# Block-sparse attention followed by a gated feed-forward layer on one core: chunks shifted by one block, opening gathers moved between queues, feed-forward units dealt by cost

## The chip, the cores and the metric

The kernel runs on one core of a Trainium2 chip. The trace names five engines with a stream of instructions each: PE (matrix products, with its weight loads as PEld), DVE (vector work), ACT (activation functions and copies), POOL (GpSimd) and SP, which here only issues transfers. Transfers are issued from the queues of SP, POOL and ACT and moved by 16 DMA engines.

The metric is the device time of one execution in microseconds (us). The kernel before was run three times: 340.7, 341.94 and 342.27 us, with the median 341.94. One further execution was profiled. Its own time was 341.41 us, and 339.6 us of it is the span that the profile shows. All times within the profile count from the start of that span.

## The reference

Inputs are q, k and v of shape (4, 8, 768, 64): 4 batches, 8 heads, 768 positions, 64 wide. A sequence has 24 blocks of 32 positions. A query block sees its own and the two neighbouring blocks, the first block (0), the last block (23), and three blocks drawn for it in `sampled_blocks`. Query blocks 0 and 23 see everything ("global" blocks, both as queries and as keys).

```python
scores = scale * np.matmul(q, k.transpose(0, 1, 3, 2))
mask = np.abs(blk_i - blk_j) <= 1
mask = mask | (blk_i == 0) | (blk_j == 0) | (blk_i == n_blocks - 1) | (blk_j == n_blocks - 1)
for qb in range(n_blocks):
    for kb in sampled_blocks[qb]:
        mask[qb * block:(qb + 1) * block, kb * block:(kb + 1) * block] = True
attn = softmax(np.where(mask, scores, -1e9))
x = np.matmul(attn, v)                  # then (3072, 512): batch and position by head and width
h = x @ w_in                            # (3072, 2048)
g = h * (1.0 / (1.0 + np.exp(-beta * h)))
out = g @ w_out                         # (3072, 512)
```

## The kernel before, in words

**Attention.** A chunk is 128 query positions, four blocks, of one batch; there are 6 chunks a batch and 24 in all. Chunk c holds blocks 4c to 4c+3, so that chunk 0 has the global block 0 and chunk 5 the global block 23. `CHUNK_ORDER` (L47 and below) visits them as 1, 2, 0, 5, 3, 4. A step is one chunk with one half of the heads (Q = 0 or 1, four heads each): 12 steps a batch, 48 steps, listed by hand in `steps`. PE, POOL and SP run in the order in which the program issues to them; DVE and ACT are reordered by a scheduler.

A step computes, for every ordinary block, a score tile of 32 queries by 256 keys: 96 neighbour keys, 32 keys of block 0, 96 drawn keys and 32 keys of block 23. `gather_chunk` lays these 256 keys side by side in a buffer KG (three buffers, `kg_bufs`): the neighbours by L248 (on ACT, on DVE in the opening), the global blocks by L253 and the drawn blocks by L259 (on POOL; the second halves of the first two chunks on DVE). `scores` (L320) multiplies, takes the row maximum on DVE (`nm`, L327) and exponentiates on ACT (`probs`, L330). `probs_T` transposes on PE (L341) and copies on DVE (L345). `attend` multiplies with the values (`av`, L392), normalises on DVE (L410, L411), and `x_transpose` (L434) builds `xT` once both halves of a chunk are done. `do_T` and `do_A` run one and two steps behind the scores.

The values lie in DRAM as a table `vtab` of 16-bit rows with all heads (1,040 bytes each). `gather_v` fetches VA (neighbours and block 0, SP's queue, L281 to L287) and VB (drawn blocks and block 23). Of VB, the blocks named in `direct` come row block by row block from SP (L291 to L297, addresses from registers), the others by an indirect gather from POOL's queue (L278). VA and VB have three buffers each, so the gather for a chunk waits until the chunk three before it has been attended.

Global query blocks are scored against all 768 keys by `global_scores` (L356) and transposed by `global_T` (L378). `attend` then multiplies them in 24 matmuls of 32 columns a step (L404), in the steps of chunk 0 and of chunk 5.

**Feed-forward ("MoE" in the code).** Chunks are collected into groups of 2, 2, 4, 4, 4, 4, 4. An h unit (`h_unit`, L448) makes 128 of the 2,048 inner columns for a group, 16 units a group; ACT takes tanh (L452) and DVE combines (L454). An o unit (`o_unit`, L465) is half of the 16 accumulating matmuls of one chunk's output; the second half is followed by a copy on ACT (L471) and the output DMA (L473). `push_group` queues a group's h units, mixed with the o units held back from earlier groups. The loop over steps deals units between the attention's instructions: as many as the queue holds divided by the steps left until the next group, rounded up.

**Opening.** SP loads k, q and v of batch 0; DVE and ACT cast; `write_vtab` writes the table (SP, 15.79 us). `prefetch_v` then fetches VA and VB of the first two chunks, with one block of each from SP and the other six by indirect gathers from POOL. POOL goes on with the loads of `w_in` (4 pieces), of k, q, v for batch 1 and of `w_out` (4 pieces), between its key copies. In step 3 the program issues two global scores, four `attend`s and the first two h units.

Of the kernel before, what the change touches and what calls it, by code (L numbers as in the profile page):

```python
# [20 lines left out]
def kernel(  # L21
# [26 lines left out]
    CHUNK_ORDER = [1, 2, 0, 5, 3, 4]  # L48
# [106 lines left out]
    def load_regs(t, engine, top, c):  # L155
        i0, i1 = max(4 * c, 1), min(4 * c + 4, NB - 1)
        _, vs = nc.values_load_multi_w_load_instructions(
            t[0:1, 3 * i0:3 * i1], engines=[engine], min_val=0, max_val=top,
            skip_runtime_bounds_check_because="block indices of the sampled blocks")
        return {(i, r): vs[3 * (i - i0) + r] for i in range(i0, i1) for r in range(3)}  # L160
# [78 lines left out]
    def gather_chunk(b, c, KG, p0, p1, eng=None, steady=False):  # L239
        eng = eng or nc.gpsimd  # L240
        js = [j for j in range(4) if 0 < 4 * c + j < NB - 1]
        j0, j1 = js[0], js[-1] + 1
        kv = kT[b]
        k_regs = load_regs(sb_raw, eng.engine, NB - 1, c)
        for w0 in range(p0, p1, 2):
            base = kv[:, w0:w0 + 2, (4 * c + j0 - 1) * BLK:(4 * c + j0 + 2) * BLK]
            ap = list(base.ap)
            (nc.scalar.copy if steady else nc.vector.tensor_copy)(  # L248
                out=KG[:, j0:j1, w0:w0 + 2, 0:96],
                in_=dataclasses.replace(base, ap=[ap[0], [BLK, j1 - j0], ap[1], ap[2]]))  # L250

        for col, src in ((96, 0), (224, S - BLK)) if chunk_seq.index((b, c)) % 6 < 3 else ():
            eng.tensor_copy(  # L253
                out=KG[:, :, p0:p1, col:col + BLK],
                in_=kv[:, p0:p1, src:src + BLK].unsqueeze(1).to_broadcast(
                    [P, 4, p1 - p0, BLK]))
        for j in js:
            for r in range(3):
                eng.tensor_copy(  # L259
                    out=KG[:, j, p0:p1, 128 + BLK * r:160 + BLK * r],  # L260
                    in_=kv[:, p0:p1, bass.ds(k_regs[(4 * c + j, r)] * BLK, BLK)])

    def gather_v(b, c, direct=()):
# [3 lines left out]
        js = [j for j in range(4) if 0 < 4 * c + j < NB - 1]  # L267
# [8 lines left out]
        for j in js:  # L276
            if j not in direct:
                nc.gpsimd.indirect_dma_start(  # L278
                    VB[:, j, :], None, tab[:, :],
                    bass.IndirectOffsetOnAxis(idx_b[:, 4 * c + j:4 * c + j + 1], 0))  # L280
        nc.sync.dma_start(out=VA[0:96, js[0]:js[0] + nj, :],  # L281
                          in_=rows((4 * c + js[0] - 1) * BLK, 96, BLK, nj))
        ga = [j for j in js if 4 * c + j != 1]
        nc.sync.dma_start(out=VA[96:128, ga[0]:ga[0] + len(ga), :],
                          in_=rows(0, BLK, 0, len(ga)))
        if len(ga) != nj:
            nc.sync.dma_start(out=VA[96:128, 1, :], in_=tab[S:S + BLK, :])  # L287
        if direct:
            v_regs = load_regs(sb_eff, ET.SP, NB, c)
            gb = [j for j in direct if 4 * c + j != NB - 2]  # L290
            nc.sync.dma_start(out=VB[96:128, gb[0]:gb[0] + len(gb), :],  # L291
                              in_=rows(S - BLK, BLK, 0, len(gb)))
            if len(gb) != len(direct):
                nc.sync.dma_start(out=VB[96:128, NB - 2 - 4 * c, :], in_=tab[S:S + BLK, :])
            for j in direct:
                for r in range(3):
                    nc.sync.dma_start(  # L297
                        out=VB[BLK * r:BLK * (r + 1), j, :],
                        in_=tab[bass.ds(v_regs[(4 * c + j, r)] * BLK, BLK), :])
# [3 lines left out]
    def scores(b, c, Q, KG):  # L303
# [6 lines left out]
        for hp in range(2):  # L310
            for pr in range(2):
                pg = 2 * Q + pr
                for j in range(4):
                    i = 4 * c + j
                    rr = slice(64 * hp, 64 * hp + 64)
                    if 0 < i < NB - 1:
                        rhs = KG[rr, j, pg, :]
                    else:
                        rhs = kT[b][rr, pg, 0:256]
                    nc.tensor.matmul(scs[hp][BLK * j:BLK * (j + 1), pr, :],  # L320
                                     lhsT=qT[b][rr, pg, i * BLK:(i + 1) * BLK],
                                     rhs=rhs, start=True, stop=True,
                                     tile_position=(64 * hp, BLK * j))
# [24 lines left out]
    def global_scores(b, Q, hp):  # L348
        rr = slice(64 * hp, 64 * hp + 64)
        halves = []  # L350
        for s in range(2):
            sct = ring.tile([P, 512], FP32, tag="bank", name="scg")[:, 0:384]
            halves.append(sct)
            for j in range(4):
                pr, blk = j // 2, (j % 2) * (NB - 1)
# [28 lines left out]
    def attend(b, c, Q, ptT, VA, VB, gTs, x16):  # L384
        av = ring.tile([P, 512], FP32, tag="bank", name="av")[:, 0:4 * VW].rearrange(
            "p (u e) -> p u e", e=VW)
        js = [j for j in range(4) if 0 < 4 * c + j < NB - 1]
# [9 lines left out]
        if len(js) < 4:  # L397
            j = 0 if c == 0 else 3
            bi = 0 if c == 0 else 1
            for u in range(4):  # L400
                pr, hp = u // 2, u % 2
                jj = 2 * pr + bi
                for ct in range(6):
                    nc.tensor.matmul(av[BLK * j:BLK * (j + 1), u, :],  # L404
                                     lhsT=gTs[hp][:, ct, BLK * jj:BLK * (jj + 1)],
                                     rhs=v16[b][:, ct, 4 * Q + u, :],
                                     start=(ct == 0), stop=(ct == 5),
                                     tile_position=(0, BLK * j))
# [51 lines left out]
    def o_unit(gi, s, part):  # L460
# [7 lines left out]
        if part == 1:  # L468
# [3 lines left out]
            r0 = b * S + c * P  # L472
            nc.scalar.dma_start(out=out[r0:r0 + P, :], in_=osb)  # L473
# [28 lines left out]


    steps = []
    for b in range(B):
        for (c, Q) in ((1, 0), (2, 0), (1, 1), (2, 1), (0, 0), (5, 0), (0, 1), (5, 1),
                       (3, 0), (3, 1), (4, 0), (4, 1)):
# [3 lines left out]
    def prep_items(b):  # L511
# [13 lines left out]
        if b == 1:  # L525
# [8 lines left out]
            for a in range(4):  # L534
                trs[5 + a] += [tr("kkqq"[a], a % 2, 0), tr("kkqq"[a], a % 2, 1)]
# [32 lines left out]
    def gather_values(n):  # L568
        if n < len(chunk_seq):
            b, c = chunk_seq[n]  # L570
            if b == 0:
                direct = {0: (1, 2, 3), 5: (0, 1, 2)}
            else:
                direct = {0: (1, 2), 5: (0, 1)}
# [25 lines left out]
    prefetch_v(0, (3,))  # L600
    prefetch_v(1, (3,))
# [42 lines left out]

    for n, (b, c, Q) in enumerate(steps):
        sidx = n % SPB
        if sidx == 0:
            prep = prep_items(b + 1) if b + 1 < B else None
        if next_group < len(groups):
            need = sum(sizes[:next_group + 1])  # L650
            gap = max(1, 2 * need + 2 - n)
        else:
            gap = max(1, len(steps) - n)
        units = -(-len(moe_q) // gap)
        pt = scores(b, c, Q, KGs[(b, c)])
        pend_T.append((b, c, Q, pt))
# [5 lines left out]
        elif n == 1:  # L662
# [4 lines left out]
            kg_half(0, 1, nc.vector)  # L667
            load_w_in(0)
# [3 lines left out]
        elif n == 2:  # L672
            do_T()
            kg_half(1, 1, nc.vector)
            load_w_in(2)
            load_w_in(3)
        elif n == 3:
# [4 lines left out]
            do_G(0, 0)  # L682
# [4 lines left out]
            do_GT()  # L687
            do_A()
            do_G(0, 1)
            do_A()  # L690
            do_X()
            do_GT()
            st_v1.append(big("st_v1"))
            run_moe(2)
# [28 lines left out]
        if n > SPB and 2 <= sidx <= 5:  # L723
            acts.append((0.55, lambda: do_G(b, sidx - 2)))
        elif n in (4, 5):
            acts.append((0.55, lambda: do_G(b, n - 2)))
        if pend_X:
            acts.append((0.85, do_X))
        done = 0
        for share, f in sorted(acts, key=lambda a: a[0]):  # L730
            upto = int(units * share + 0.5)
            run_moe(upto - done)
            done = upto
            f()
        run_moe(units - done)
# [44 lines left out]
```

## Time and profile before

| | |
|---|---|
| median of three runs | 341.94 us |
| the profiled execution | 341.41 us, of which 339.6 us are the span |
| PE busy | 292.8 us (86%), 4,288 matmuls |
| DVE, ACT, POOL busy | 222.4, 225.7, 174.3 us |
| DMA | 56.95 MB, 168 GB/s over the span |
| granted TensorE clock | 0.979 of full speed over the span |

The costliest groups of instructions, with the line, the engine, the operation, `out<-in`, the count, busy time in all and mean ns of one, and the idle time of the engine before them:

```profile
L448 PE MATMUL hps<-xT,w_in_sb 128*128 128x512 f16 (+1 forms) x448 | 99.2, 360 | 1.9 <-DVE gnm L366 0.7
L465 PE MATMUL ops<-w_out_sb,g 128*128 128x512 f16 x384 | 89.6, 379 | 3.8 <-DMA w_out_sb<-in_moe_w_out_dram 3.8
L259 POOL COPY KG<-kT 128x128 f16 (+1 forms) x264 | 62.8, 293 | 3.0 <-PE sc L320 1.9
L248 ACT COPY KG<-kT 128x768 f16<-128x768 f16 (+1 forms) x44 | 34.6, 793 | 11.3 <-PE sc L320 7.1
```

The mean of a matmul counts its way through the pipeline: eight matmuls of 512 columns in a row take 1.73 us, not eight times 360 ns. A slice of the page is 339.6 / 40 = 8.5 us.

### The profile page before, as it was taken

What the parts mean: (1) busy time and instruction counts of PE and PEld (TensorE: products, weight loads), DVE (VectorE), ACT (ScalarE), POOL (GpSimd) and SP (SyncE); (2) the same over time, 40 slices, a digit from 0 to 9 for tenths busy, and PEclk for the clock granted to TensorE, in tenths of its full rate; (3) what the DMA queues carried; (4) which work ended last, traced back from release to release, by engine and by line L of the source; (5) the groups of instructions that cost most, each with busy time, mean ns of one, the idle gap of its engine ahead of it and who ended that gap; (6) DMA issues with size and microseconds to landing.
All of it is one profiled execution on the core that took longest, in us unless ns stands there. A gap on an engine that the chain in (4) does not pass through costs nothing.

```text
span 339.6 us, 11327 instructions
## 1 busy us (share of the span) xinstructions
PE 292.8 (86%) x4288; PEld 166.1 (49%) x4288; DVE 222.4 (65%) x506; ACT 225.7 (66%) x447; POOL 174.3 (51%) x451
## 2 busy tenths in 40 slices
PE   0554898669787999887999999999989999899995
PEld 0342556545555565544455565454555554444442
DVE  3666878624859777899686668677997576534400
ACT  1693579943768799887688987667776545335411
POOL 5659985629889955879696519725131200000000
PEclk9999999979969999999799999999999999999999
DMA  6979999997698992659898327724162510000021
GB/s 169 377 230 202 292 252 326 274 225 239 169 286 207 314 268 51 173 137 294 183 306 251 75 68 191 178 59 115 35 184 68 135 57 33 31 33 31 32 93 64
DMA packets 40135, 56.95 MB, mean 168 GB/s; under 512 B 7280, under 2 KB 31984, under 8 KB 40080
## 3 DMA queue, kind: packets, MB, share of 16 engines
q0 software_dynamic: 10160, 26.21, 29.2%
q1 hardware_dynamic: 24400, 23.71, 25.7%
q10 hardware_dynamic: 5520, 6.30, 5.4%
q8 instruction: 34, 0.56, 0.7%
q14 instruction: 21, 0.17, 0.2%
HBM read 50.77 MB, written 9.62 MB: 178 GB/s over the span
## 4 chain that ended last, share of the span: by engine, by line
PE 57%; DVE 14%; DMA 10%; ACT 10%; issue 3%; POOL 3%; SPq 1%; another core or an unknown queue 0%; POOLq 0%; DVEq 0%; ACTq 0%
PE ops L465 21%; PE hps L448 19%; PE tp_p L341 5%; ACT probs L330 5%; DVE nm L327 4%; DVE g L454 4%; DMA w_out_sb<-in_moe_w_out_dram 4%; DMA st_kq<-in_k_dram 4%; PE sc L320 3%; PE av L392 3%; DMA st_q<-in_q_dram 3%; ACT t_sb L452 2%; PE av L404 2%; DVE gnm L364 2%; PE tp_x L434 1%
## 5 line engine op out<-in xcount | busy, mean ns | idle before, releaser
L448 PE MATMUL hps<-xT,w_in_sb 128*128 128x512 f16 (+1 forms) x448 | 99.2, 360 | 1.9 <-DVE gnm L366 0.7
L454 DVE SCALAR_TENSOR_TENSOR g<-t_sb,hps 128x512 f16<-128x512 f16 (+1 forms) x112 | 66.8, 609 | 46.9 <-ACT t_sb L452 44.2
L465 PE MATMUL ops<-w_out_sb,g 128*128 128x512 f16 x384 | 89.6, 379 | 3.8 <-DMA w_out_sb<-in_moe_w_out_dram 3.8
L452 ACT ACTIVATE t_sb<-hps,beta_h_sb 128x512 f16<-128x512 f32 (+1 forms) x112 | 70.3, 647 | 29.4 <-PE hps L448 26.4
L330 ACT ACTIVATE probs<-sc,nm 128x256 f16<-128x256 f32 x192 | 76.9, 485 | 18.2 <-DVE nm L327 14.3
L327 DVE TENSOR_REDUCE nm<-sc 128x2 f32<-128x512 f32 x96 | 62.9, 684 | 20.0 <-PE sc L320 16.5
L278 POOL DMA_INDIRECT VB<-vtab,idx_b x40 | 38.9, 972 | 71.5 <-PE av L392 55.9
L259 POOL COPY KG<-kT 128x128 f16 (+1 forms) x264 | 62.8, 293 | 3.0 <-PE sc L320 1.9
L448 PEld LDWEIGHTS <-w_in_sb 128*128 128x128 f16 x448 | 42.8, 101 | 35.3 <-issue 5.2
L465 PEld LDWEIGHTS <-g 128*128 128x128 f16 x384 | 36.8, 98 | 45.8 <-issue 4.7
L248 ACT COPY KG<-kT 128x768 f16<-128x768 f16 (+1 forms) x44 | 34.6, 793 | 11.3 <-PE sc L320 7.1
L345 DVE COPY probsT<-tp_p 128x1024 f16<-128x1024 f16 x48 | 32.3, 673 | 4.8 <-PE hps L448 1.7
L341 PE MATMUL tp_p<-identity,probs 128*128 128x128 f16 x384 | 32.2, 231 | 1.2 <-ACT probs L330 0.6
L471 ACT ACTIVATE osb<-ops 128x512 f32<-128x512 f32 x24 | 14.4, 601 | 28.0 <-PE ops L465 27.9
L320 PE MATMUL sc<-KG,qT 64*32 64x256 f16 x704 | 25.0, 294 | 7.5 <-DVE KG L259 5.1
L341 PEld LDWEIGHTS <-probs 128*128 128x128 f16 x384 | 23.9, 103 | 5.2 <-issue 2.0
L392 PEld LDWEIGHTS <-probsT 128*32 128x32 f16 x1408 | 17.4, 100 | 18.1 <-issue 14.1
L369 ACT ACTIVATE gp<-scg,gnm 128x384 f16<-128x384 f32 x32 | 16.9, 581 | 13.7 <-DVE gnm L366 7.5
L392 PE MATMUL av<-VA,probsT 128*32 128x65 f16 x704 | 22.1, 203 | 2.8 <-issue 2.7
L392 PE MATMUL av<-VB,probsT 128*32 128x65 f16 x704 | 21.8, 201 | 2.9 <-DMA VB<-vtab 2.2
L411 DVE TENSOR_TENSOR x<-av,rec 128x256 f16<-128x256 f32 x48 | 20.1, 420 | 0.8
L207 PE MATMUL tp_k<-identity,k 128*128 128x128 f16 x96 | 9.1, 242 | 12.3 <-ACT k L200 12.1
(69 smaller groups left out, 280.1 us busy)
## 6 DMA issues: line engine op xcount, KB each, us to landing
VA<-vtab SPq DMA_DIRECT2D x16, 390.0 KB
out_dram<-osb ACTq DMA_DIRECT2D x24, 256.0 KB
VB<-vtab SPq DMA_DIRECT2D x147, 32.5 KB
st_k<-in_k_dram POOLq DMA_DIRECT2D x6, 768.0 KB
st_q<-in_q_dram POOLq DMA_DIRECT2D x6, 768.0 KB, 9.3
st_v<-in_v_dram POOLq DMA_DIRECT2D x6, 768.0 KB, 9.7
VA<-vtab SPq DMA_DIRECT2D x8, 292.5 KB
vtab<-v POOLq DMA_DIRECT2D x3, 780.0 KB
```

The costliest lines, as they stand in the source:

```text
L248: (nc.scalar.copy if steady else nc.vector.tensor_copy)(out=KG[:, j0:j1, w0:w0 + 2, 0:96], in_=dataclasses.replace(base, ap=[ap[0], [BLK, ...
L259: eng.tensor_copy(out=KG[:, j, p0:p1, 128 + BLK * r:160 + BLK * r], in_=kv[:, p0:p1, bass.ds(k_regs[(4 * c + j, r)] * BLK, BLK)])
L278: nc.gpsimd.indirect_dma_start(VB[:, j, :], None, tab[:, :], bass.IndirectOffsetOnAxis(idx_b[:, 4 * c + j:4 * c + j + 1], 0))
L320: nc.tensor.matmul(scs[hp][BLK * j:BLK * (j + 1), pr, :], lhsT=qT[b][rr, pg, i * BLK:(i + 1) * BLK], rhs=rhs, start=True, stop=True, tile_ ...
L327: nc.vector.tensor_reduce(out=nm[:, hp, :], in_=scs[hp], axis=AX.X, op=ALU.max, negate=True)
L330: last_exp[0] = nc.scalar.activation(out=pt[:, 2 * pr + hp, :], in_=scs[hp][:, pr, :], func=AF.Exp, bias=nm[:, hp, pr:pr + 1], scale=1.0)
L341: nc.tensor.transpose(out=tp[:, u * 256 + half * P:u * 256 + (half + 1) * P], in_=pt[:, u, half * P:(half + 1) * P], identity=identity)
L392: nc.tensor.matmul(av[BLK * j:BLK * (j + 1), u, :], lhsT=ptT[:, u, half, BLK * j:BLK * (j + 1)], rhs=V[:, j, h * VW:(h + 1) * VW], start=( ...
L448: nc.tensor.matmul(hp[:, 0:n], lhsT=w_in_sb[:, cc, f * P:(f + 1) * P], rhs=xT_tiles[gi][:, cc, 0:n], start=(cc == 0), stop=(cc == N_DMC - 1))
L452: nc.scalar.activation(out=t_sb[:, 0:n], in_=hp[:, 0:n], func=AF.Tanh, bias=0.0, scale=beta_h_sb[:, f:f + 1])
L454: nc.vector.scalar_tensor_tensor(out=g_tiles[gi][:, f, 0:n], in0=t_sb[:, 0:n], scalar=1.0, in1=hp[:, 0:n], op0=ALU.add, op1=ALU.mult)
L465: nc.tensor.matmul(op, lhsT=g_tiles[gi][:, f, s * P:(s + 1) * P], rhs=w_out_sb[:, f, :], start=(f == 0), stop=(f == N_FFC - 1))
```

## The change

Chunk c now holds blocks 4c-1 to 4c+2. Chunk 0 is blocks 23, 0, 1, 2: both global query blocks and two ordinary ones; chunks 1 to 5 are ordinary. They are visited as 1, 2, 3, 4, 5, 0. In `attend` both global blocks of a head go through one matmul of 64 columns in place of two of 32. Chunk 0's output leaves in two DMAs.

In batch 0 the neighbour keys are no longer copied; the score matmul of a block is split into one of 96 columns on `kT` and one of 160 on KG.

In the opening the first two chunks' VB comes wholly from SP, the second halves of their keys are gathered by POOL, one piece of `w_in` is loaded before the values, and the rest of `w_in` and the k loads of batch 1 come after the key gathers. In batch 0 three blocks each of chunks 3 and 4 and two of the others come from SP; in the later batches two blocks of chunks 1 to 5 and one of chunk 0.

The global scores of batch 0 move from steps 3, 4, 5 to steps 4, 5, 10, 11; in later batches they come one step earlier. Units are dealt by cost: a target of columns accumulates over the steps, and the queue is to last one step longer than before.

```diff
-    CHUNK_ORDER = [1, 2, 0, 5, 3, 4]
+    CHUNK_ORDER = [1, 2, 3, 4, 5, 0]
...
-        js = [j for j in range(4) if 0 < 4 * c + j < NB - 1]
+        js = [2, 3] if c == 0 else [0, 1, 2, 3]
...
-        for w0 in range(p0, p1, 2):
-            base = kv[:, w0:w0 + 2, (4 * c + j0 - 1) * BLK:(4 * c + j0 + 2) * BLK]
+        for w0 in range(p0, p1, 2) if b > 0 else ():
+            base = kv[:, w0:w0 + 2, (4 * c + j0 - 2) * BLK:(4 * c + j0 + 1) * BLK]
...
-                    i = 4 * c + j
+                    i = (4 * c + j - 1) % NB
                     rr = slice(64 * hp, 64 * hp + 64)
-                    if 0 < i < NB - 1:
-                        rhs = KG[rr, j, pg, :]
+                    if c == 0 and j < 2:
+                        parts = [(0, 256, kT[b][rr, pg, 0:256])]
+                    elif b == 0:
+                        parts = [(0, 96, kT[b][rr, pg, (i - 1) * BLK:(i + 2) * BLK]),
+                                 (96, 256, KG[rr, j, pg, 96:256])]
                     else:
-                        rhs = kT[b][rr, pg, 0:256]
+                        parts = [(0, 256, KG[rr, j, pg, :])]
...
-        if len(js) < 4:
-            j = 0 if c == 0 else 3
-            bi = 0 if c == 0 else 1
+        if c == 0:
             for u in range(4):
                 pr, hp = u // 2, u % 2
-                jj = 2 * pr + bi
                 for ct in range(6):
-                    nc.tensor.matmul(av[BLK * j:BLK * (j + 1), u, :],
-                                     lhsT=gTs[hp][:, ct, BLK * jj:BLK * (jj + 1)],
+                    nc.tensor.matmul(av[0:2 * BLK, u, :],
+                                     lhsT=gTs[hp][:, ct, 2 * BLK * pr:2 * BLK * (pr + 1)],
                                      rhs=v16[b][:, ct, 4 * Q + u, :],
                                      start=(ct == 0), stop=(ct == 5),
-                                     tile_position=(0, BLK * j))
+                                     tile_position=(0, 0))
...
+    def moe_cost(f, a):
+        return 8 * D_MODEL if f is o_unit else N_DMC * max(320, P * len(groups[a[0]]))
+    moe_done = [0.0]
+    def run_moe_to(target):
+        while moe_q:
+            cost = moe_cost(*moe_q[0])
+            if moe_done[0] + 0.5 * cost > target:
+                break
+            run_moe(1)
+            moe_done[0] += cost
...
-        for (c, Q) in ((1, 0), (2, 0), (1, 1), (2, 1), (0, 0), (5, 0), (0, 1), (5, 1),
-                       (3, 0), (3, 1), (4, 0), (4, 1)):
+        for (c, Q) in ((1, 0), (2, 0), (1, 1), (2, 1), (3, 0), (4, 0), (3, 1), (4, 1),
+                       (5, 0), (5, 1), (0, 0), (0, 1)):
...
-                direct = {0: (1, 2, 3), 5: (0, 1, 2)}
+                direct = {0: (2, 3), 3: (0, 1, 2), 4: (0, 1, 2)}
             else:
-                direct = {0: (1, 2), 5: (0, 1)}
+                direct = {0: (2,)}
             prefetch_v(n, direct.get(c, (0, 1)))
...
     write_vtab(0, nc.sync)
-    prefetch_v(0, (3,))
-    prefetch_v(1, (3,))
+    load_w_in(0)
+    prefetch_v(0, (0, 1, 2, 3))
+    prefetch_v(1, (0, 1, 2, 3))
...
-            gap = max(1, 2 * need + 2 - n)
+            gap = max(1, 2 * need + 2 - n) + 1
...
-        units = -(-len(moe_q) // gap)
+        target0 = moe_done[0] + moe_carry
+        budget = max(0.0, sum(moe_cost(*u) for u in moe_q) - moe_carry) / gap
...
-            kg_half(0, 1, nc.vector)
-            load_w_in(0)
+            kg_half(0, 1)
+        elif n == 2:
+            do_T()
+            kg_half(1, 1)
             load_w_in(1)
             load_quad("k", k, 1, 0, None, nc.gpsimd)
             load_quad("k", k, 1, 1, None, nc.gpsimd)
-        elif n == 2:
-            do_T()
-            kg_half(1, 1, nc.vector)
             load_w_in(2)
             load_w_in(3)
...
-            do_G(0, 0)
             do_A()
             pend_A.rotate(-1)
             do_A()
             do_T()
-            do_GT()
+            do_X()
             do_A()
-            do_G(0, 1)
             do_A()
-            do_X()
-            do_GT()
             st_v1.append(big("st_v1"))
-            run_moe(2)
...
-        if n > SPB and 2 <= sidx <= 5:
-            acts.append((0.55, lambda: do_G(b, sidx - 2)))
-        elif n in (4, 5):
-            acts.append((0.55, lambda: do_G(b, n - 2)))
+        g_steps = (4, 5, 10, 11) if b == 0 else (1, 2, 3, 4)
+        if sidx in g_steps:
+            acts.append((0.45, lambda: do_G(b, g_steps.index(sidx))))
...
-        done = 0
         for share, f in sorted(acts, key=lambda a: a[0]):
-            upto = int(units * share + 0.5)
-            run_moe(upto - done)
-            done = upto
+            run_moe_to(target0 + share * budget)
             f()
-        run_moe(units - done)
+        run_moe_to(target0 + budget)
+        moe_carry = target0 + budget - moe_done[0] if moe_q else 0.0
```

## The prediction

> **What bounds the kernel now.** I read the page's slices first, then windows of ten microseconds, then the waits of PE and of SP, then the timeline at the places these point to.
>
> ```profile
> PE   0554898669787999887999999999989999899995
> DVE  3666878624859777899686668677997576534400
> ACT  1693579943768799887688987667776545335411
> PEclk9999999979969999999799999999999999999999
> DMA  6979999997698992659898327724162510000021
> ```
> ```profile
> 60.00:70.00 10.00, 6.04 (x110) 4.51 (x109) 5.46 (x14) 9.32 (x19) 5.11 (x14) 1.00 1.16 260
> 90.00:100.00 10.00, 6.33 (x118) 4.10 (x118) 5.65 (x14) 6.45 (x16) 8.22 (x17) 0.66 0.93 259
> 140.00:150.00 10.00, 7.81 (x172) 4.66 (x158) 9.22 (x20) 7.70 (x17) 8.66 (x28) 1.00 0.55 140
> 180.00:190.00 10.00, 10.00 (x176) 6.05 (x174) 7.46 (x16) 8.98 (x16) 7.22 (x17) 1.00 0.80 230
> ```
> From 160 us on PE has no gap to speak of: there the end moves only by PE work. Before that PE loses time for changing reasons: transfers (60 to 70), a slow clock and late operands (90 to 100), a full DVE (140 to 150). PE's order is fixed, so a microsecond lost early comes out at the end, unless a later loss shrinks.
>
> Adding PE's matmuls at their closest spacing (0.216 us for 512 columns, 0.109 for 256, 0.0575 for a transpose, 0.36 for 16 score matmuls, 0.35 for an `av` of 32, 0.71 for the 24 of L404) gives 264 us of work. Step 12, the first of batch 1, starts its scores at 87.00 with 40 us of it done (47 lost); step 28 starts at 168.3 with 102 done (19 more lost); after that 5.6 are lost.
>
> ```profile
> PE sc L320 <- DVE KG L259: 5.1, 2, 4.1
> PE ops L465 <- DMA w_out_sb<-in_moe_w_out_dram: 3.8, 3, 3.0
> PE av L392 <- DMA VB<-vtab: 2.2, 1, 2.2
> ```
> ```profile
> SPq L297 <- DMA VA<-vtab: 12.7, 10, 2.5
> ```
> The opening waits on DVE's key copies (32.43), on a value gather (63.99) and on `w_out` (67.76, 71.77). SP waits in turn for its own transfers: each of its DMAs waits for the semaphore of the one eight before it, so at most eight are in flight.
>
> ```profile
> 35.47 9.80 SPq L297 DMA_DIRECT2D VB<-vtab  x9
> 42.09 1.03 POOL L278 DMA_INDIRECT VB<-vtab,idx_b  x1 [0.16 <-PE tp_x L434]
> 51.89 0.76 POOL L176 DMA_DIRECT2D w_out_sb<-in_moe_w_out_dram  x1
> 63.62 1.49 POOL L176 DMA_DIRECT2D w_out_sb<-in_moe_w_out_dram  x2
> ```
> Nine row gathers took 9.80 us here; the free ones of step 12's time took 2.90 for six. The last of the `w_out` pieces, issued at 64.36, landed at 77.17, 12.81 us later (the chain of waits has this piece), and step 10 follows it by 4.7.
>
> **The change part by part.**
>
> *Global queries in one chunk.* L404 has 384 matmuls of 128x32, in 16 bursts of 24. It keeps 192, in 8 bursts, each 64 columns wide:
> ```profile
> 57.85 0.80 PE L404 MATMUL av<-v,gpT 128*32 128x65 f16 x21
> ```
> A step with such a burst spends 1.10 us between its first `av` and its next transpose (57.48 to 58.58), one without 0.39 (84.76 to 85.15): 0.71 us a burst. A 128-column weight load with 128 moving columns runs at 0.0575, so one of 64 columns fits into the 0.0296 of these; I keep the price. Before step 12 the old order has done four bursts, the new one none, so behind it 12 become 8: 4 x 0.71 = -2.8 us (bounds -2.8 and, if 64-wide ones cost twice, +2.8).
> The new bursts stand behind `av` of 128x32 tiles. A step's `av` ends 0.2 us after its issue; one such drain for each of 8 bursts would be 1.6 us. The Trainium skill, TensorEngine Tiling (Array Packing), Key Properties, says that changing the tiling mode drains TensorE, where until now both had the same mode. By that rule the sum below is 1.6 us longer; it is not in the sum.
>
> *Score halves read in place (batch 0).* 176 matmuls more, 32 a step. The 96 and 160 columns of one block share a column group, so they follow each other and keep the next block waiting: some 0.64 + 0.07 us a step against 0.36, 12 x 0.35 = 4.2 us at most, 0 at least. All of it lies before step 12, where PE waits for VB and `w_out` anyway: I take 0 there; without that cover it costs the 4.2. It takes from ACT 8 of the 44 copies of L248 (0.793 each, 6.3 us) and from DVE 4; ACT is 93% busy between 60 and 70, but what ends the waits there is a transfer.
>
> *Key copies on POOL.* The 24 copies L259 and 4 of L253 leave DVE. On POOL a half-gather took 2.86 us (15.67 to 18.53). Keys of the second half are ready at 21.85, so POOL is done with both at about 27.7, against DVE's last at 32.58. Step 3's scores come at 28.2, not 32.43: 4.2 us gained, if the values are there.
>
> *Value gathers of the opening.* They are not. SP now issues 12 row gathers for each of the first two chunks (3 before), and 9 for each of the next two. The first chunk: issue from 23.89 at 0.51 to 0.75, last at about 30.9, landed 33 (before, PE came to it at 34.91). The second: 520 KB, and the 520 KB of its VA part, start at 31.2 beside POOL's loads (`w_in` and k, 28 to 32, as before at 29 to 34). What SP's queue moved beside POOL's loads: 292 KB between landings at 50.76 and 54.12, 87 GB/s; 292 KB between 42.81 and 46.58, 77; but 747 KB from the issue at 30.5 to 46.58, 47, with gaps for the eight semaphores. At 80 the 1.04 MB take 13 us; with 1.3 for the last it lands at 45.5 (47 GB/s: 53; VA's first 390 KB alone, 3.08 us or 127 GB/s: 40). I take 45.5, since fewer loads compete: `w_in`'s first piece goes out at 19, and six indirect gathers (780 KB) are gone. PE waits there from about 35, and step 4's scores, behind it in PE's order, start near 47.5 (44.7 before).
> Behind it on POOL: the two indirect gathers of the fifth chunk reuse the second chunk's buffer, so they wait for that `av` (46.5; before 42.09), and with them the k casts, q and v loads and `w_out`. By POOL's rows: 46.5, gathers 2.6, cast 2.2, q load 0.8, so q lands at 57.8 (5.7 after issue, as the v load at 94.29 did; 9.6 under load); cast, `w_out`, six copies, cast, and the last two pieces go at 65.2. Landings at 2.5 us a load and 2.7 to 3.9 a piece: 78.4 for the last, +1.2. Step 10 follows by 4 matmuls, 12 transposes, one o unit, 3.6 in all; steps 10 and 11 (now with an o unit, two h units and both global scores) take 7.5 where they took 5.2. Step 12: 78.4 + 3.6 + 7.5 = 89.5, **+2.5 us**. A landing at 53 makes it +10.0; one at 40 only +0.3, since five load issues at 0.8, 36 key copies at 0.24 and two indirect gathers at 1.3 keep POOL until 44.3. With two h units more done, 8 x 0.109 = -0.9.
>
> *MoE dealt by cost.* Three late steps have no h or o unit and run at their latency: step 26 takes 4.4 us with 1.9 of work, 34 takes 2.8 with 2.1, 42 takes 3.2 with 1.8: 4.6 lost. Now the queue lasts one step longer and every step from 19 on has units; I take two thirds, **-3.1** (bounds 0 and -4.6).
>
> *Output.* Chunk 0 is written by two DMAs, and it is the last one: one more issue of 0.34 behind the last `osb`, +0.3.
>
> **Sum.** 339.6 + 2.5 - 0.9 - 2.8 - 3.1 + 0.3 = 335.6 us of span. The profiled run took 341.41 (1.81 around the span); the median of the runs is 0.53 above it. 335.6 + 1.81 + 0.53 = **337.9 us**.
>
> **Rivals.**
> *The opening starves (slower).* SP's queue gets the 47 GB/s that it had from 30.5 to 46.58; the second chunk's values land at 53, POOL and `w_out` follow 7.5 later, step 12 starts at 97.0. 339.6 + 10.0 - 0.9 - 2.8 - 3.1 + 0.3 = 343.1, on the runs' scale 345.4. For it: the 9.80 us line, in which eight transfers in flight did not fill the queue. Against: the loads ahead of POOL's end are one piece shorter than before. Slower than before it is from a landing at 49.5 on.
> *The opening is fed (faster).* SP's queue gets 110 to 127 GB/s, as the first VA had; landing at 40 to 41, then POOL decides: step 12 at 87.3, 333.4, or 335.7. For it: little is in flight from 25 to 29. Against: 77 to 87 is the best that a row beside loads shows. The Trainium skill, DMA: Bandwidth & Descriptors, Queues, rings and completion order, says that each DMA engine goes round the queues packet by packet; by it SP's rows of 1,040 bytes beside pieces of 2,048 would get a third of some 330 GB/s, which is this case. With 47 to 87 the trace agrees only in part.
> *The dealing does more (faster).* PE's gaps between 90 and 110 and between 140 and 160 are 9.9 us by the windows. If evenly dealt units fill half of them, 5.0 more go: 330.6, or 332.9. For it: PE's clock is granted 0.66 in 90 to 100, so that a filled gap pays twice. Against: DVE is over 90% busy in 140 to 160.
> *The dealing does nothing.* An h unit costs DVE 0.69 as before, and evenly dealt units wait for DVE (78 to 97% busy from 130 to 160). Then the -3.1 falls away: 338.7, or 341.0, no change that can be told.
>
> **How the numbers follow.** Forecast 0.36 (own range 334 to 341), starved 0.25, more 0.15, idle dealing 0.14, fed 0.10. Half a per cent, 1.7 us, is about what can be told from no change, so faster is below 340.2 and slower above 343.7. Faster, same, slower: forecast 0.30, 0.05, 0.01; more 0.15; fed 0.09, 0.01; idle dealing 0.03, 0.08, 0.03; starved 0.01 same, 0.24 slower: 0.57, 0.15, 0.28. The range 328 to 346 leaves out the far ends of starved and of more.
>
> **What would show it.** Right: PE waits from about 35 to 46 in `av` for VB, no wait of `sc` for DVE; the last `w_out` lands near 78; step 12's scores at 88 to 91; no step from 19 on without h or o; L404 with 192 matmuls. Wrong: `av` waiting past 50 or not at all; step 12 before 86 or after 94; gaps between 90 and 160 larger than the 19 us lost now; L404 bursts above 0.8 us.

## The result, and the profile after

The changed kernel takes 362.21 us (median of 4 runs, 359.63 to 366.34), the kernel before, on the same chip, 342.11 us. The ratio is 1.0568, 95% interval [1.0457, 1.0680]: slower by 19 us, where 337.9 us and a gain were forecast. The run of 366.34 us was in a slower state of the chip and is left out of the ratio, as such runs are below. The profiled execution took 359.63 us with a span of 357.9 us (before: 341.41 and 339.6).

First scores of a step, us from the start of the span, read from the trace:

| | before | after |
|---|---|---|
| step 12 (batch 1 begins) | 87.0 | 96.1 |
| step 12 to step 28 | 81.3 | 85.0 |
| step 28 to the end | 171.3 | 176.8 |

Nine microseconds are lost in the opening and nine more behind it. The slices of the page after (8.9 us each):

```profile
PE   0563347877897948979797699899999999999995
DVE  3552216863989853889887267767787775343400
ACT  2682006797788666978878398767766754354411
PEclk9995558899999987999999899999999999999999
DMA  6998987999599788249956813554146401011021
```
PE now falls to 3 in slices 4 and 5, and it has holes at slices 15 (a 4) and 23 (a 6), where before it was at 9. Its clock is granted at 0.50 from slice 4 into slice 7, so the first work behind the wait runs at half clock; no run separates what that adds. In the windows (PE busy and its count, PEld, DVE, ACT, POOL, then clock, DMA share, GB/s) they stand out:

```profile
40.00:50.00 10.00, 0.89 (x7) 0.42 (x7) 0.60 (x2) 0.00 (x0) 4.79 (x17) 0.50 1.14 246
60.00:70.00 10.00, 7.17 (x96) 5.43 (x96) 7.50 (x18) 5.92 (x15) 3.05 (x6) 0.83 1.04 332
90.00:100.00 10.00, 8.86 (x178) 5.75 (x178) 9.38 (x24) 7.87 (x19) 7.34 (x19) 1.00 0.61 147
130.00:140.00 10.00, 4.81 (x77) 3.29 (x78) 3.36 (x8) 4.56 (x10) 9.09 (x19) 0.66 0.75 192
140.00:150.00 10.00, 9.16 (x163) 5.33 (x162) 6.84 (x14) 9.41 (x19) 5.61 (x14) 1.00 0.46 138
190.00:200.00 10.00, 5.65 (x94) 3.37 (x93) 5.17 (x10) 6.51 (x14) 6.75 (x18) 1.00 0.73 217
```
The waits of PE and of SP after (us in all, times, longest), and the timeline at the places shown of before:

```profile
PE av L398 <- DMA VB<-vtab: 11.9, 6, 4.3
PE tp_k L208 <- POOL k L201: 10.2, 2, 5.8
PE sc L326 <- POOL KG L261: 3.9, 8, 1.7
PE ops L469 <- DMA w_out_sb<-in_moe_w_out_dram: 3.9, 2, 2.3
SPq L299 <- DMA VA<-vtab: 6.1, 3, 2.9
```
```profile
35.47 11.13 SPq L299 DMA_DIRECT2D VB<-vtab  x12
51.47 0.96 POOL L280 DMA_INDIRECT VB<-vtab,idx_b  x1 [5.04 <-DMA VA<-vtab]
61.17 0.76 POOL L177 DMA_DIRECT2D w_out_sb<-in_moe_w_out_dram  x1
75.77 1.48 POOL L177 DMA_DIRECT2D w_out_sb<-in_moe_w_out_dram  x2
```
The opening is late the way the prediction's chain has it: the second chunk's values land at 50.07, POOL's gathers for the fifth chunk go at 51.47 instead of 42.09, and the last `w_out` piece goes out at 76.50 instead of 64.36 and lands at 85.07; step 12 follows 11.0 later. The two transfers in the chain that ended last (start and duration):

```profile
46.29 3.78 DMA VB<-vtab
76.50 8.57 DMA w_out_sb<-in_moe_w_out_dram
```
But the second wait, `tp_k` for casts on POOL, was in no list of before. POOL's largest group in the page after:

```profile
L261 POOL COPY KG<-kT 128x128 f16 (+1 forms) x288 | 67.8, 293 | 17.9 <-issue 10.2
```
The key copies cost what they did (293 ns each), but POOL stands idle 17.9 us ahead of them (3.0 before), mostly for "issue", that is for nothing that the page can name. Right ahead of them in its queue are register loads. `gather_chunk` and `gather_v` call `load_regs` once each; before and after (minimum, median and maximum in ns; the view of that one line, first before, then after):

```profile
L157 POOLq TENSOR_LOAD <-sb_raw x24: 806/820/2098, 5.5 to 251.1; - x24
L157 SPq TENSOR_LOAD <-sb_eff x24: 744/758/1901, 21.9 to 267.9; - x24
```
```profile
L158 POOLq TENSOR_LOAD <-sb_raw x26: 1388/2730/5182, 5.5 to 268.4; - x26
L158 SPq TENSOR_LOAD <-sb_eff x24: 1264/2476/3464, 21.8 to 282.9; - x24
```
Except for chunk 0's, a load has become about three times as long, for twelve registers as before (the last chunk's nine are now twelve, too). Chunk 0's load six instead of nine and give the minima. Summed over all loads, that is 49 us more in POOL's queue (74.9 against 25.6) and 34 us more in SP's (58.2 against 24.2). Some loads take longer still, up to 5.18 us; what adds to those isn't shown. The diff has the reason in a line that the prediction passed over:

```diff
     def load_regs(t, engine, top, c):
-        i0, i1 = max(4 * c, 1), min(4 * c + 4, NB - 1)
+        i0, i1 = max(4 * c - 1, 1), 4 * c + 3
         _, vs = nc.values_load_multi_w_load_instructions(
             t[0:1, 3 * i0:3 * i1], engines=[engine], min_val=0, max_val=top,
```
Chunk c's registers began at element 12c (byte 48c); now they begin at 12c - 3 (byte 48c - 12). Before, chunk 0 alone began at element 3, and its nine registers took 1.87 us on SP and 2.06 to 2.10 on POOL, while every other chunk's nine or twelve took 0.75 and 0.82.

How this reaches PE: the stretch before the 5.85 us wait, on POOL and PE, after.

```profile
122.94 1.88 POOL L201 CAST k<-st_k 128x384 f16<-128x384 f32 x4
125.12 0.76 POOL L87 DMA_DIRECT2D st_q<-in_q_dram  x1 [0.30 <-POOL k L201]
128.74 2.91 POOL L261 COPY KG<-kT 128x128 f16 x12 [2.86 <-PE av L398]
131.78 1.02 POOL L280 DMA_INDIRECT VB<-vtab,idx_b  x1
133.11 1.00 POOL L280 DMA_INDIRECT VB<-vtab,idx_b  x1 [0.30 <-issue]
134.09 1.87 POOL L201 CAST k<-st_k 128x384 f16<-128x384 f32 x4
135.13 1.71 PE L208 MATMUL tp_k<-identity,k 128*128 128x128 f16 x12 [5.85 <-POOL k L201]
```
Between the q load (125.12) and the key copies (128.74) POOL does nothing but one register load of 3.45 us, which ends at 128.5:

```profile
L158 POOLq TENSOR_LOAD <-sb_raw x1: 3451/3451/3451, 125.1 to 125.1; - x1
```
The page puts that gap down to an `av`, which only happens to end there: with short loads (experiment 1) the same copies run five microseconds ahead of that `av`. Everything behind it is late, and last the second cast, for which PE's transposes stand in its fixed order.

**Theory:** the moved register loads cost most of the 19 us. **Rival 1:** the opening does, since 24 row gathers pass through SP, eight in flight. **Rival 2:** the dealing of units and the place of batch preparation do.

### The profile page after: what moved, and what is told of

It is laid out like the page before. It is cut to its first block, busy times and chain, and to the rows that moved or that the text cites. A ratio compares the mean times of both kernels' runs of the same rounds, so it can differ in the third digit from the quotient of the medians.

```text
span 357.9 us, 11275 instructions
## 1 busy us (share of the span) xinstructions
PE 289.7 (81%) x4272; PEld 165.9 (46%) x4272; DVE 215.9 (60%) x474; ACT 220.7 (62%) x439; POOL 178.0 (50%) x476
## 4 chain that ended last, share of the span: by engine, by line
PE 59%; DMA 13%; POOL 6%; issue 6%; ACT 5%; DVE 5%; SPq 4%; POOLq 1%; ACTq 0%
PE ops L469 20%; PE hps L452 20%; PE tp_p L347 5%; DMA VB<-vtab 4%; PE av L398 4%; PE sc L326 3%; DMA st_v<-in_v_dram 3%; DMA w_out_sb<-in_moe_w_out_dram 2%; ACT probs L336 2%; DMA VA<-vtab 2%; PE av L408 2%; SPq L158 2%; DMA vtab<-v 1%; POOL VB L280 1%; POOL KG L261 1%
## 5 line engine op out<-in xcount | busy, mean ns | idle before, releaser
L452 PE MATMUL hps<-xT,w_in_sb 128*128 128x512 f16 (+1 forms) x448 | 97.8, 356 | 4.3 <-ACT gp L375 2.1
L469 PE MATMUL ops<-w_out_sb,g 128*128 128x512 f16 x384 | 90.9, 383 | 4.6 <-DMA w_out_sb<-in_moe_w_out_dram 3.9
L456 ACT ACTIVATE t_sb<-hps,beta_h_sb 128x512 f16<-128x512 f32 (+1 forms) x112 | 68.4, 642 | 33.4 <-PE hps L452 28.4
L261 POOL COPY KG<-kT 128x128 f16 (+1 forms) x288 | 67.8, 293 | 17.9 <-issue 10.2
L280 POOL DMA_INDIRECT VB<-vtab,idx_b x37 | 36.0, 974 | 52.1 <-PE av L398 40.7
L398 PE MATMUL av<-VB,probsT 128*32 128x65 f16 x704 | 23.5, 200 | 14.3 <-DMA VB<-vtab 11.9
L398 PEld LDWEIGHTS <-probsT 128*32 128x32 f16 x1408 | 18.7, 99 | 31.9 <-issue 20.0
L250 ACT COPY KG<-kT 128x768 f16<-128x768 f16 (+1 forms) x36 | 28.4, 805 | 6.0 <-PE sc L326 5.2
L326 PE MATMUL sc<-KG,qT 64*32 64x256 f16 (+1 forms) x704 | 23.7, 277 | 3.9 <-POOL KG L261 3.9
L255 POOL COPY KG<-kT 128x512 f16<-128x512 f16 (+1 forms) x28 | 15.0, 566 | 19.6 <-ACT kT L212 7.5
```

The lines of the kernel that those rows point to most:

```text
L261: eng.tensor_copy(out=KG[:, j, p0:p1, 128 + BLK * r:160 + BLK * r], in_=kv[:, p0:p1, bass.ds(k_regs[(4 * c + j - 1, r)] * BLK, BLK)])
L280: nc.gpsimd.indirect_dma_start(VB[:, j, :], None, tab[:, :], bass.IndirectOffsetOnAxis(idx_b[:, 4 * c + j - 1:4 * c + j], 0))
L326: nc.tensor.matmul(scs[hp][BLK * j:BLK * (j + 1), pr, w0:w1], lhsT=qT[b][rr, pg, i * BLK:(i + 1) * BLK], rhs=rhs, start=True, stop=True, t ...
L398: nc.tensor.matmul(av[BLK * j:BLK * (j + 1), u, :], lhsT=ptT[:, u, half, BLK * j:BLK * (j + 1)], rhs=V[:, j, h * VW:(h + 1) * VW], start=( ...
L452: nc.tensor.matmul(hp[:, 0:n], lhsT=w_in_sb[:, cc, f * P:(f + 1) * P], rhs=xT_tiles[gi][:, cc, 0:n], start=(cc == 0), stop=(cc == N_DMC - 1))
L456: nc.scalar.activation(out=t_sb[:, 0:n], in_=hp[:, 0:n], func=AF.Tanh, bias=0.0, scale=beta_h_sb[:, f:f + 1])
```

## The experiments

Each ratio is against the kernel before on the same chip, with its 95% interval.

**1. The changed kernel with its register loads aligned again.**

```diff
-    sb_raw = persist.tile([1, NB * 3], I32, name="sb_raw")
-    nc.vector.tensor_copy(out=sb_raw, in_=sb_i32[0:1, :, 0])
+    sb_raw = persist.tile([1, NB * 3 + 8], I32, name="sb_raw")
+    nc.vector.memset(sb_raw[:, 0:3], 0)
+    nc.vector.tensor_copy(out=sb_raw[:, 3:3 + NB * 3], in_=sb_i32[0:1, :, 0])
...
-        i0, i1 = max(4 * c - 1, 1), 4 * c + 3
+        i0, i1 = 4 * c - 1, 4 * c + 3
...
-            t[0:1, 3 * i0:3 * i1], engines=[engine], min_val=0, max_val=top,
+            t[0:1, 3 * i0 + 3:3 * i1 + 3], engines=[engine], min_val=0, max_val=top,
```
`sb_eff` is treated in the same way.

> The changed kernel with three leading elements in both index tiles and every register load reading twelve elements from 12c again (48c bytes), nothing else. Theory (the moved register loads): the loads fall from 2.5 us (SP) and 2.7 us (GpSimd) to the 0.75 and 0.82 us they took before; SP's row gathers of the second chunk land 3 to 4 us earlier than 50.1, and the time falls from 362 to 338 to 346 us. Rival 1 (the opening starves because 24 row gathers go through SP, eight in flight): at most 4 us come back, 357 to 361. Rival 2 (the dealing and the preparation steps, which leave TensorE waiting for key casts): at most 5, 356 to 361.

Measured: 1.0123 [1.0078, 1.0167], 344.28 us. The loads, and the stretch that waited before:

```profile
L160 POOLq TENSOR_LOAD <-sb_raw x26: 806/817/2002, 5.5 to 253.4; - x26
L160 SPq TENSOR_LOAD <-sb_eff x24: 745/752/1507, 21.2 to 267.7; - x24
```
```profile
120.00 0.76 POOL L87 DMA_DIRECT2D st_q<-in_q_dram  x1 [0.30 <-POOL k L203]
120.97 2.91 POOL L263 COPY KG<-kT 128x128 f16 x12 [0.22 <-issue]
126.34 1.87 POOL L203 CAST k<-st_k 128x384 f16<-128x384 f32 x4
127.42 0.50 PE L210 MATMUL tp_k<-identity,k 128*128 128x128 f16 x6
```
Key copies follow the q load after 0.97 us instead of 3.62, and the transposes come without a wait. From 1.0568 to 1.0123 some 15 us are back, against 4 or 5 by the rivals. By the profiles, step 12 still starts at 95.3 (96.1), but from there to the end it takes 247.5 us instead of 261.8. So the loads are the loss behind the opening. With this opening they hardly move step 12; with the old one they do (3 and 4).

**2. The kernel before with misaligned loads.** One leading element in both index tiles (`3 * i0 + 1:3 * i1 + 1`), nothing else.

> The kernel before with one leading element in both index tiles, so that every register load starts at 48c + 4 bytes, as the changed kernel's do modulo 16; nothing else. Theory: the loads rise to 2.5 and 2.7 us and the time from 342 to 350 to 362. Rivals 1 and 2: the loads may get longer, but the time stays at 341 to 344, since nothing of the opening or the dealing has changed.

Measured: 1.0260 [1.0218, 1.0302], 348.13 us.

```profile
L159 POOLq TENSOR_LOAD <-sb_raw x24: 822/2713/4473, 5.5 to 256.4; - x24
L159 SPq TENSOR_LOAD <-sb_eff x24: 752/2470/3030, 21.1 to 273.1; - x24
```
The rivals fall as explanations of this part: the kernel before loses 8.8 us to four bytes, a little under the range given. Its order hides more of the loads than the new one does (PE waits 2.6 us for casts on POOL between 87 and 173, after: 10.2 in all). The minima are chunk 0's, which now start at element 4, on 16 bytes.

**3 and 4. The opening of before,** in the changed kernel as it is and in the one with aligned loads.

```diff
-    load_w_in(0)
-    prefetch_v(0, (0, 1, 2, 3))
-    prefetch_v(1, (0, 1, 2, 3))
+    prefetch_v(0, (3,))
+    prefetch_v(1, (3,))
...
-            kg_half(0, 1)
+            kg_half(0, 1, nc.vector)
+            load_w_in(0)
+            load_w_in(1)
+            load_quad("k", k, 1, 0, None, nc.gpsimd)
+            load_quad("k", k, 1, 1, None, nc.gpsimd)
-            kg_half(1, 1)
-            load_w_in(1)
-            load_quad("k", k, 1, 0, None, nc.gpsimd)
-            load_quad("k", k, 1, 1, None, nc.gpsimd)
+            kg_half(1, 1, nc.vector)
```


> The changed kernel, register loads as they are (off 16 bytes), with the opening of the kernel before: one row of each of the first two chunks gathered directly and three by indirect DMA, second-half key copies on VectorE, load order as before. Rival 1: step 12 starts at 86 to 89 instead of 96.1, and the time is 351 to 355. Theory: the long loads stay in GpSimd's and SP's queues; the opening gains at most half of the 9 us, 356 to 362.

> Both: the aligned register loads of the first kernel and the opening of the kernel before. Theory: within 3 us of the first kernel of this set, either way, 337 to 345. Rival 1: 6 to 9 us below the first kernel of this set.

Measured: 1.0476 [1.0437, 1.0514] with the long loads, 0.9971 [0.9947, 0.9995] with short ones. Rival 1 is right for a part: the new opening costs 1.5% (5.2 us) with short loads and 0.9% (3.1 us) with long ones. But its forecast for 3 failed: the time, 356.04 us, is at the edge of the theory's range, and step 12 starts at 95.97, hardly before the 96.1 of the changed kernel. With short loads it starts at 90.3, and the last `w_out` piece lands at 78.28 instead of 80.75. So with the old opening the long loads put off step 12 by 5.7 us, with the new one by 0.8: the two losses overlap. For 4 neither range of the difference held: it is 5.3 us below experiment 1, between the theory's 3 and the rival's 6 to 9. With both undone, the change is 0.3% faster than before, by less than the half per cent that counts as a difference.

**5. Neighbour copies again in batch 0,** on top of 4 (`for w0 in range(p0, p1, 2):`, and no split of the scores).

> The version with aligned loads and the old opening, and in addition the 96 neighbour columns of batch 0 copied into the key tile again, so that each block's scores are one matmul of 256 columns. If the split scores cost PE what I bounded them with (0.35 us a step, 4.2 us over the 12 steps of batch 0), step 12 starts 2 to 4 us earlier than 90.3 and the ratio to before falls from 0.997 to 0.985 to 0.99. If the opening covers them, as the prediction took it, step 12 stays within 1 us of 90.3 and the ratio within 0.994 to 1.002; more copies on ACT and DVE can then only cost.

Measured: 0.9963 [0.9931, 0.9996], step 12 at 90.2. No difference that can be told from 4: the opening covers what the split costs. At full clock the 32 score matmuls of a step start within 0.24 us, the 16 unsplit ones within 0.16, and from a step's first score to PE's next instruction it is 0.40 against 0.36: 0.04 us a step, not the 0.35 that bounded it.

**6. Units dealt by count,** on top of 4.

```diff
-            gap = max(1, 2 * need + 2 - n) + 1
+            gap = max(1, 2 * need + 2 - n)
...
+        units = -(-len(moe_q) // gap)
+        done = 0
         for share, f in sorted(acts, key=lambda a: a[0]):
-            run_moe_to(target0 + share * budget)
+            upto = int(units * share + 0.5)
+            run_moe(upto - done)
+            done = upto
             f()
-        run_moe_to(target0 + budget)
+        run_moe(units - done)
```


> The version with aligned loads and the old opening, with the MoE units dealt by count, rounded up, over one step less, as before. Theory (dealing by cost is worth the 3.1 us predicted): step 12 to the end takes 250 to 252 us instead of 248.0, ratio 1.003 to 1.009. Rival (the dealing does nothing): 247 to 249, ratio 0.995 to 0.999. Rival 2 (it harms): below 246, ratio below 0.992.

Measured: 1.0183 [1.0143, 1.0224], against 0.9971. The dealing by cost, with the queue lasting one step longer, is worth 2.1% (7 us) of the timed runs, more than the range given; against 5, which ran on the same chip, it is 2.2%. Its profiled execution was the shortest of its runs, and there step 12 to the end takes 251.4 against 248.0, so 3.4 us; but 5, dealt like 4, takes 250.6 there, so a single pair of profiles can't size it. The late steps without h or o unit are the same as before (26, 34 and 42); dealt by cost there is none from step 19 on. Both rivals fall: the dealing gains.

**7. The k loads of batch 1 later,** on top of 1 (moved from step 2 to step 3, behind the second indirect gather).

> The changed kernel with aligned loads (new opening), with the two k loads of batch 1 (0.79 MB each) issued behind the second indirect gather, near 39, instead of near 28. If GpSimd's loads beside it hold SP's queue down (60 GB/s from 31 to 48), the second chunk's last row lands at 43 to 45.5 instead of 48.2, and step 4 starts 2 to 4 us earlier; the time falls by 1 to 4 us unless q and w_out land later. If the limit is SP's own eight transfers in flight, it lands at 47 or later.

Measured: 1.0188 [1.0131, 1.0245]; the second chunk's last row lands at 50.17, later than the 48.2. A miss: the larger VA transfer in front of these rows lands at 40.2 as before. The k loads are out of its way, but two pieces of `w_in` now go out where they did (27.2 and 28.0), and the k loads, issued at 38.0, run beside the rows. "47 or later" was the forecast for a limit by the eight transfers in flight; as the collision only moved, the run doesn't decide between the two.

**8. Offsets of 8 and 12 bytes.** The kernel before with two leading elements in POOL's tile and three in SP's.

> The kernel before with two leading elements in GpSimd's index tile and three in SP's, so that the loads of chunks 1 to 5 start 8 and 12 bytes off a multiple of 16. If a load is quick only from a multiple of 16 bytes: 2.4 to 2.8 us for both queues, and quick only where the start falls on 16 bytes again. If 8 bytes were enough, GpSimd's stay at 0.82 and only SP's rise. The rows of the first chunk (9 registers) start at 3 + 2 and 3 + 3 elements, 4 and 8 bytes off.

Measured (a single run, 347.07 us):

```profile
L159 POOLq TENSOR_LOAD <-sb_raw x24: 2059/2716/4664, 5.4 to 256.9; - x24
L159 SPq TENSOR_LOAD <-sb_eff x24: 1864/2470/3039, 21.0 to 273.6; - x24
```
Eight bytes don't do. The minima are loads of nine registers (the first and the last chunk), which are off 16 bytes here as well.

**9 and 10. All of `w_out` ahead of the v loads,** on top of 4 and on top of 1.

```diff
-                         cast("k", 1), load("q", 1), load_v1]
-            items[5] += [w[0]]
-            items[6] += [cast("q", 0), w[1]]
-            items[7] += [cast("q", 1), w[2], w[3]]
+                         cast("k", 1), load("q", 1)] + w + [load_v1]
+            items[6] += [cast("q", 0)]
+            items[7] += [cast("q", 1)]
```


> The version with aligned loads and the old opening, with the four w_out pieces issued ahead of batch 1's two v loads instead of between the q casts (54.9, 62.1, 66.5, 67.3 there). If step 12 follows the last w_out piece, that piece lands at 72 to 75 instead of 78.3, step 12 starts at 86 to 88 instead of 90.3, and the ratio to before falls from 0.997 to 0.985 to 0.992. If step 12 is set by PE's own work and clock by then, it stays at 89 to 91 and the ratio at 0.995 to 0.999; the v loads that now come later may then cost 1 to 3 us behind step 12.

> The changed kernel with aligned loads (new opening) and the same edit. If its late step 12 (95.3) comes through GpSimd's queue to w_out (last piece landing at 82.9), as the prediction's mechanism has it, the last piece lands at 76 to 78, step 12 starts at 90 to 92 and 3 to 5 us of the 5.3 that the opening costs come back (ratio 1.00 to 1.004). If the values of the chunks themselves hold it (step 4 at 50.5 and av waiting for VB), step 12 stays above 94 and the ratio above 1.008.

Measured: 0.9988 [0.9961, 1.0015] and 1.0078 [1.0041, 1.0115]. Step 12 does move with `w_out`, to 85.3 (from 90.3) and 91.2 (from 95.3), with the last piece at 73.84 and 77.58. So waiting for `w_out` holds up step 12 in both openings. It is not what sets them apart: step 12 is still 5.9 us later with the new opening (5.0 without this edit), though PE waits for no piece of `w_out` in 10. The distance is there from step 4 on (50.06 against 42.05), behind the values. The late values delay PE by its fixed order, which alone keeps the 5.9 us here, and `w_out` by POOL's queue, which ends last without this edit.

The ratios forecast for an earlier step 12 were both missed, since the time hardly follows: step 12 to step 16 takes 26.8 and 24.9 us instead of 22.4 and 19.8. In both, PE pauses there in the bursts of global queries (in 9 in `tp_p` too), and then its clock is granted at 0.50 for 6.8 us, from 94.5 in 9 and from 98.3 in 10:

```profile
93.44 0.23 PE L410 MATMUL av<-v,gpT 128*64 128x65 f16 x2 [0.51 <-issue]
94.19 0.27 PE L410 MATMUL av<-v,gpT 128*64 128x65 f16 x3 [0.52 <-issue]
94.96 0.29 PE L410 MATMUL av<-v,gpT 128*64 128x65 f16 x2 [0.50 <-issue]
```
(these lines are of 9). What ends these pauses the profile doesn't show, and I didn't try it.

**11. Only GpSimd's loads aligned** in the changed kernel (`sb_raw` shifted by three, `sb_eff` as it was).

> The changed kernel with only GpSimd's index tile shifted by three, so that its loads are aligned (0.82 us) and SP's are not (2.5 us). Theory: GpSimd's queue carries most of the loss, because the key casts that PE waited for at 135 and 199 are behind its loads: the two long waits of tp_k for GpSimd go, and the time falls from 362 to 345 to 351. If SP's queue carries it: 355 to 361.

Measured: 1.0097 [1.0061, 1.0132], no worse than with both aligned (1.0123 [1.0078, 1.0167]).

```profile
L160 POOLq TENSOR_LOAD <-sb_raw x26: 807/816/1994, 5.2 to 253.7; - x26
L160 SPq TENSOR_LOAD <-sb_eff x24: 1266/2478/3370, 21.4 to 268.3; - x24
```
So the whole loss from the loads, 15 us, is on POOL's queue, and PE's waits in `tp_k` for POOL fall from 10.2 to 0.3 us. SP's loads take 60.0 us here against 19.6 in experiment 1, and these 40 us cost nothing that the runs can tell.

**12. The kernel before with chunk 0's loads aligned too** (`i0 = 4 * c`, twelve registers from element 0).

> The kernel before with one edit: the register loads of the first chunk start at element 0 (12 registers, block 0's three unused) instead of element 3 (9 registers, 1.9 to 2.1 us). Theory: these eight loads fall to 0.75 to 0.85 us. GpSimd's four save 4.9 us of its queue; all 26 loads of the changed kernel gave 15 us of time for some 49 us of queue, so about a third of it, 0.5 to 1.6 us, comes out at the end: ratio 0.995 to 0.999. If these four stand where nobody waits for GpSimd: 0.999 to 1.001.

Measured: 1.0011 [0.9983, 1.0039]. Chunk 0's loads fall to 0.81 to 0.84 us on POOL and 0.75 on SP, and no gain shows; by the interval it is 0.6 us at most. That fits the second forecast, that these few stood where nobody waited for POOL.

## Why the prediction was wrong, by its own steps

| term | predicted | measured |
|---|---|---|
| register loads | no term | +15 us, on POOL's queue (1, 11) |
| opening, step 12 | +2.5, step 12 at 89.5 | at 96.1; 95.3 with short loads, 5.2 us of time (1, 4) |
| global queries | -2.8 | about -0.4 |
| split scores | 0, price up to 4.2 | 0 (5) |
| dealing by cost | -3.1 | -3.4 in the profiles, -7 in the timed runs (6) |

**The step that failed** is "The change part by part": its sum has no term for the register loads. It priced the gathers' issues, copies and transfers, but not the line of `load_regs` in the diff, which moves the start of the same slice by three elements. The price stood in the profile of before, in the spread of one row: 0.75 us for most loads, 1.9 for those of chunk 0. Neither the forecast nor a rival had it, so the range, with 346 at its upper end, could not hold the time. The term explains most of the miss, not all of it: with short loads the kernel takes 344.28 us, inside the range, but still slower than before and close to the 345.4 of the starved rival, not a gain.

**The opening** was mis-sized, and its chain is not the only way to the late step 12. The second chunk's values were to land at 45.5 at 80 GB/s. They landed at 50.07 in the changed kernel and at 48.17 with short loads; 1.04 MB from the VA issue at 30.82 on is 60 GB/s. So it lay between forecast and starved rival, close to the break-even of 49.5. POOL followed later than I took it, too: the last `w_out` piece landed at 85.07 (82.88 with short loads), not 78.4. The last term held in the changed kernel: from that landing to step 12 I had 11.1 us, and it took 11.0. But with `w_out` moved out of the way step 12 stays as late against the old opening (9 and 10), by PE's own order behind the values, of which the sum has no term. POOL's second-half keys did bring step 3's scores forward (first at 25.5, before 27.6), to no use, since PE then waited for values until 50.2. The fed rival is out: over this stretch SP's queue got 55 to 60 GB/s, not its 110 to 127.

**Global queries:** the matmuls were halved, as told:

```profile
L408 PE MATMUL av<-v,gpT 128*64 128x65 f16 x192 | 7.8, 196 | 1.4 <-issue 1.4
```
The price of a burst was not kept. The 0.71 came from one step of 1.10 us; most steps with a burst are shorter. At full clock such a step takes 0.98 us between its first `av` and the next transpose before, 1.23 after, one without 0.39: 12 x 0.59 = 7.1 against 8 x 0.84 = 6.7. Of this, the way from the first `av` to the first global matmul is 0.15 before (after 24 `av`) and 0.35 after (after only 16). These 0.20 us for each of 8 bursts are the 1.6 us that the prediction named and left out. The Trainium skill, TensorEngine Tiling (Array Packing), Key Properties, says that TensorE drains when the tiling mode changes; here the trace agrees with it.

**The dealing** was right in direction and at least in size, its late steps are filled as forecast, and the split scores were covered as claimed. With loads and opening put back, the time from step 12 to the end falls from 252.6 to 248.0; the steps before it lose 3.3, since global scores and an o unit now stand there and `w_out` lands 1.1 later. What is left is the 0.3%. Undone in the order of the experiments, the loads are 15.2 us, the opening 5.2 and the rest -1.0, which is 19.4 us (0.0568 x 342) by construction. In the other order the opening is 3.1 and the loads 17.3: some 2 us come back only with both undone.

## What to carry to other kernels

When a diff moves an index, follow every slice made from it, also that of a register load, whose price hangs on its start and not only on its length; pad the tile or load a few registers more so that it starts on a multiple of 16 bytes. A row whose maximum is far above its median can hold such a price (2098 against 820 here), though not always: with all loads aligned one still takes 2002. Ask which of its calls are the long ones, and whether it is always the same ones, before the change makes all of them so. And ask which queue carries a delay: here the same 1.7 to 1.9 us a gather cost 15 us on one queue and nothing on the other, because PE's fixed order waits for casts that stand behind the first.

## What was not expected of the hardware

Register loads, by registers and start (SP / POOL, us): from a multiple of 16 bytes, nine or twelve registers 0.75 / 0.82; off it by 4, 8 or 12 bytes six take 1.26 / 1.39, nine 1.87 / 2.06, twelve 2.47 / 2.72. That is 0.2 us a register off 16 bytes. On 16 bytes, nine cost the same as twelve, as if four came at a time; that is a reading, only the durations are shown. The Trainium skill, Runtime: NRT & Kernel Launch, Instruction fetch mechanics, gives some 200 ns a register even in bulk; that page has loads from HBM in view, and these read SBUF. The trace agrees off 16 bytes (2.47 / 12 = 0.21) and not on them (0.75 / 12 = 0.06); there the measurement decides.
